# Four score banks of each middle block exponentiated on VectorE instead of ScalarE

## The chip, the cores and the metric

The kernel runs on one core of a Trainium2 chip. The metric is the device time of one execution in microseconds. A core has TensorE (PE) for matrix products, ScalarE (ACT) for activation functions, VectorE (DVE) and GpSimd (POOL) for elementwise work, and SyncE (SP), which here issues the DMAs. PE writes only to PSUM, which has 8 banks of 128 x 512 float32; the other data lie in SBUF.

## The reference

x is 2048 x 448 (bfloat16), with 16 heads of 28, a dense layer of 1792 in between, and an output of the same shape as x.

```python
def _A_ref(x, wqkv, wo):
    H = 16; Dh = D // H
    q, k, v = ...                      # x @ wqkv, split by heads
    scores = jnp.einsum("bhqd,bhkd->bhqk", q, k) * Dh ** -0.5
    p = _softmax(scores, axis=-1)
    o = jnp.einsum("bhqk,bhkd->bhqd", p, v)
    return o.transpose(0, 2, 1, 3).reshape(B, S, D) @ wo

def _B_ref(x, w1, b1, w2, b2):
    h = _gelu(jnp.einsum("bsd,df->bsf", x, w1) + b1)
    return jnp.einsum("bsf,fd->bsd", h, w2) + b2

xn = _layernorm(x)
return x + _A_ref(xn, wqkv, wo) * _silu(_B_ref(xn, w1, b1, w2, b2))
```

## The kernel before

**Attention.** The 16 heads form 4 groups of 4 (G), the 2048 queries 4 chunks of 512 (C), the 2048 keys 16 tiles of 128 (T). A *block* is one group with one chunk, 16 blocks in all. A block has 64 score *banks*, numbered m: 16 key tiles by 4 heads, each 128 keys x 512 queries. In all there are 1024 banks. The last block is cut into four quarters of the queries.

Banks are taken in *units*: pairs in block 0, threes afterwards (UB = 3). For each unit, `p_scores` (L903) has PE write its scores into the ring, 6 PSUM banks, so two units of three fit; `p_exps` (L932) has ACT exponentiate the whole unit in one instruction into slots of P (21 slots in SBUF); `p_pv` (L969) has PE multiply these with V, adding into the PSUM bank acc over the 16 key tiles. V has a column of twos, which gives the softmax denominators. No maximum is subtracted per row; a bound on the scores is folded into q and k. At the end of a block `p_epi` copies acc to SBUF on DVE (L1016), takes reciprocals (L1026) and multiplies them in (L1045), with small matmuls between.

**Filling.** One PSUM bank, misc, is left for everything else once PV has started. Through it go, tile by tile, the projections of k and q (`t_proj` L591; DVE evictions L602, L747, L757), of v (L771, L781), the first dense layer (`p_f1`: PE L811, DVE L824, 56 tiles), the second (`p_f2`: PE L854, DVE L859, 16 tiles), and the output projection (L1055, DVE L1064 and L1066). When all 56 tiles of the first layer are there, ACT runs gelu over them in four instructions (L836). `p_silu` gives the gate by a tanh on ACT (L868) and a product on DVE (L871). The output is projection x gate (L1064) plus x (L1066), then stored from SP.

**Order.** Every engine has one fixed order of instructions, laid out by a planner before the run. Each process (`p_...`) is a generator that yields tasks with an engine, buffers read and written, a planned duration and a rank; the planner puts next what can start first, and among tasks of one engine that can start within 0.1 us of one another the one of lowest rank. Scores have rank 1, exponentials 3, evictions of the first layer 2, PV 6 (1.2 when it lags more than four units), filling matmuls 5. `deps` turns the buffers into semaphore waits: an instruction waits for the last write of what it reads, and for the last write and all reads since of what it writes. What PE itself wrote is not waited for on PE. x stays in SBUF from the load at the start (`x_sb`) until L1066.

Of the kernel before, what the change touches and what calls it, by code (L numbers as in the profile page):

```python
# [6 lines left out]
dt = mybir.dt  # L7
ACTF = mybir.ActivationFunctionType
ALU = mybir.AluOpType
# [5 lines left out]
D = 448  # L15
# [4 lines left out]
C = 4  # L20
# [4 lines left out]
UB = 3  # L25
NRING = 6
NP = 21
NBLK = G * C
MTOT = NBLK * T * 4

UNITS = []
for _m in range(0, 64, 2):
    UNITS.append(([_m, _m + 1], _m % 4, _m % 20))
for _m in range(64, MTOT, UB):
    UNITS.append((list(range(_m, _m + UB)), (_m - 64) % NRING, (_m - 64) % NP))
NU = len(UNITS)
RB = {m: b0 + k for ms, b0, p0 in UNITS for k, m in enumerate(ms)}
PB = {m: p0 + k for ms, b0, p0 in UNITS for k, m in enumerate(ms)}
SM_SCALE = DH ** -0.5
LN_EPS = 1e-5  # L40
KNORM = 2.5
PV_START = 8
# [26 lines left out]
class _Kernel:  # L69
# [164 lines left out]
    def alloc(self):  # L234
# [57 lines left out]
        self.b_acc, self.b_misc = B(), B()  # L292
        self.b_P = [B() for _ in range(NP)]
        self.b_x = [B() for _ in range(C)]
        self.b_xn = [[B() for _ in range(4)] for _ in range(3)]
        self.b_xnT = [[B(), B()] for _ in range(C)]
        self.b_wqkf = B()
# [24 lines left out]
        self.b_rf = [B(), B()]  # L322
        self.banks = [(self.misc[:, :], self.b_misc), (self.acc[:, :], self.b_acc)]
        self.s_x = [self.sem("s_x%d" % q) for q in range(4)]
        self.s_out = [self.sem("s_out%d" % q) for q in range(10)]
        self.s_w = {n: self.sem("s_" + n) for n in ("wqk", "wv", "w1", "w2", "wo", "b")}

    def schedule(self):
        K = self
        K.n_f1 = 0  # L330
        K.exp_u = -1
        K.sc_u = -1
        K.pv_u = -1
        K.E_done = -1
        K.norms_done = False
        K.stg_done = 0
        K.qsqs = [0, 1]
# [9 lines left out]
        K.ring_busy = [False] * NRING  # L347
        K.P_busy = [False] * NP
# [12 lines left out]
        K.spawn(K.p_exps(), 0)  # L361
        K.spawn(K.p_pv(), 0)
        o = 1.0
# [500 lines left out]
    def p_silu(self, c):  # L864
        K = self
        yield ("until", lambda: K.f2n[c] == 4 and K.ready([K.b_fsb[c % 2]], 0.3) and (c < 2 or K.g_done[c - 2]))
        fb, sg = K.fsb[:, c % 2, :, :], K.sig[:, c % 2, :, :]
        yield _Task(ACT, lambda eng: eng.activation(sg, fb, ACTF.Tanh, scale=0.5),  # L868
                    [K.b_fsb[c % 2]], [K.b_sig[c % 2]], 1.6, 0.0, 0)
        for t in range(4):  # L870
            yield _Task(DVE, lambda eng, t=t: eng.scalar_tensor_tensor(K.g_sb[:, c, t, :], sg[:, t, :], 1.0, fb[:, t, :],  # L871
                                                                       op0=ALU.add, op1=ALU.mult),
                        [K.b_sig[c % 2], K.b_fsb[c % 2]], [K.b_h[c], K.b_g[c]], 0.63, 0.0, 6)
        K.g_done[c] = True

    def pieces(self, m):
        b, r = m // 64, m % 64
# [11 lines left out]
    def p_scores(self):  # L889
        K = self  # L890
        for u in range(NU):
            ms = UNITS[u][0]
            fl, rd = [], []
            ps = [(m,) + K.pieces(m) for m in ms]
            for k in range(4):
                for m, b, j, pc, _, _ in ps:
                    if k >= len(pc):
                        continue
                    t, q0, nq, col = pc[k]
                    g, c = b // C, b % C  # L900

                    def f(eng, m=m, t=t, j=j, g=g, c=c, q0=q0, nq=nq, col=col):
                        return eng.matmul(K.ring[:, RB[m], col:col + nq],  # L903
                                          K.kT[32 * j:32 * j + 32, g, t * 128:(t + 1) * 128],
                                          K.qT[32 * j:32 * j + 32, g, c * 512 + q0:c * 512 + q0 + nq],
                                          tile_position=(32 * j, 0), start=True, stop=True)
# [11 lines left out]
            yield ("until", lambda: not any(K.ring_busy[RB[m]] for m in ms))  # L918
            yield _Task(PE, fall, rd, [K.b_ring[RB[m]] for m in ms], 0.17 + 0.05 * len(ms) + 0.02 * (len(fl) - len(ms)), 0.1, 1)
            for m in ms:  # L920
                K.ring_busy[RB[m]] = True
            K.sc_u = u

    def p_exps(self):
        K = self
        for u in range(NU):
            ms, b0, p0 = UNITS[u]
            n = len(ms)
            yield ("until", lambda: K.sc_u >= u and not any(K.P_busy[p0 + k] for k in range(n)))

            def fexp(eng, b0=b0, p0=p0, n=n):
                return eng.activation(K.P[:, p0:p0 + n, :], K.ring[:, b0:b0 + n, :], ACTF.Exp, scale=SM_SCALE)  # L932
            yield _Task(ACT, fexp, [K.b_ring[b0 + k] for k in range(n)], [K.b_P[p0 + k] for k in range(n)],
                        0.0843 + 0.4267 * n, 0.08, 3)
            for k in range(n):
                K.ring_busy[b0 + k] = False
                K.P_busy[p0 + k] = True
            K.exp_u = u
            if u >= NU - 2:
                for k in range(n):  # L940
                    K.banks.append((K.ring[:, b0 + k, :], K.b_ring[b0 + k]))

    def p_pv(self):
        K = self
# [2 lines left out]
        K.banks.pop(i)  # L947
        K.pv_started = True
        for u in range(NU):
            ms = UNITS[u][0]  # L950
            parts, cur = [], []
            for m in ms:
                cur.append(m)
# [4 lines left out]
            for part in parts:  # L958
                if not part:
                    continue  # L960
                first = K.sub_of(part[0])
                yield ("until", lambda: K.exp_u >= u and K.E_done >= first - 1)
                fl, rd = [], []
                for m in part:
                    b, j, pc, end, s = K.pieces(m)
# [15 lines left out]
                yield _Task(PE, fall, rd, [K.b_acc], 0.18 + 0.05 * len(part) + 0.02 * (len(fl) - len(part)), 0.1,  # L981
                            lambda: 1.2 if K.exp_u - K.pv_u > 4 else 6)
                for m in part:
                    K.P_busy[PB[m]] = False
# [75 lines left out]
    def t_oev(self, ps, tok, c, t):  # L1060
# [2 lines left out]
        wr = K.b_osb[c][t // 2] if c < C - 1 else K.b_o4[t]  # L1063
        yield _Task(DVE, lambda eng: eng.tensor_tensor(o, ps, K.g_sb[:, c, t, :], ALU.mult),  # L1064
                    [tok, K.b_g[c]], [wr], 0.63, 0.0, 3)
        yield _Task(DVE, lambda eng: eng.tensor_tensor(o, o, K.x_sb[:, c, t, :], ALU.add),  # L1066
                    [K.b_x[c], wr], [wr], 0.4, 0.0, 3)
# [78 lines left out]
```

## Time and profile before

| | |
|---|---|
| median of 3 runs | 531.56 us (528.48 to 532.66) |
| the profiled execution | 530.83 us, its span 529.0 us |
| mean granted PE clock | 0.894 |
| busy, PE / DVE / ACT / POOL | 466.3 / 172.5 / 502.8 / 64.1 us |
| exponentials on ACT | 352 instructions, 461.8 us |
| gelu on ACT | 4 instructions, 24.4 us |
| DMA | 9.13 MB |

The page of the profile is one execution of the program. Busy time counts overlapping instructions of one engine once, so a group's busy time can be less than its count times its mean. The forty slices are the span in equal parts of 13.2 us, with the busy share in tenths. A group of instructions is given by source line, engine, operation and tile, with busy us, the mean ns of one, and the idle time of the engine just before it with what ended it. `acc<-P,vaug` means that acc is written from P and vaug.

### The profile page before, as it was taken

The numbers are of one execution on the slowest core, as the hardware profiler recorded it, in microseconds if no ns is written. First come the engines' busy times: TensorE is split into PE (matmuls) and PEld (weight loads), VectorE is DVE, ScalarE is ACT, GpSimd is POOL, SyncE is SP. The second block draws the span as 40 slices with busy tenths as digits, with TensorE's granted clock in tenths as the row PEclk, the third lists the DMA queues.
The fourth block names the chain that finished last, engine by engine and source line by source line (L and its number), as shares of the span: only waits on it lengthen the run. The fifth ranks groups of instructions, "written<-read, shape, count | busy, mean of one in ns | idle before, by whom it ended". The sixth has DMA issues, their size and how long they took to land.

```text
span 529.0 us, 8343 instructions
## 1 busy us (share of the span) xinstructions
PE 466.3 (88%) x3478; PEld 149.9 (28%) x3507; DVE 172.5 (33%) x304; ACT 502.8 (95%) x385; POOL 64.1 (12%) x93
## 2 busy tenths in 40 slices
PE   6899899899989999989976799999878889898984
PEld 2433233222222222222221333333212112121542
DVE  6823433343433343343433132313400003031244
ACT  3898999999999999999999799999999999999993
POOL 5662101210101001010111001000101000010100
PEclk9999999999999999999995999999955558566698
DMA  8800000000000000000000000000000000000010
GB/s 238 245 16 18 0 1 1 0 1 1 1 1 1 0 1 2 1 1 1 0 1 0 0 2 1 1 0 1 1 0 2 0 1 35 1 14 22 2 46 27
DMA packets 7925, 9.13 MB, mean 17 GB/s; under 512 B 2384, under 2 KB 6928, under 8 KB 7888
## 3 DMA queue, kind: packets, MB, share of 16 engines
q1 hardware_dynamic: 7888, 8.61, 5.3%
q8 instruction: 27, 0.44, 0.3%
q14 instruction: 10, 0.08, 0.0%
HBM read 6.77 MB, written 1.84 MB: 16 GB/s over the span
## 4 chain that ended last, share of the span: by engine, by line
ACT 44%; PE 36%; issue 14%; DVE 5%; ACTq 0%; DVEq 0%
ACT P L932 44%; PE ring L903 8%; PE misc L854 8%; PE acc L969 7%; PE misc L591 3%; PE misc L1055 2%; PE acc L678 2%; PE misc L771 1%; PE misc L1040 1%; DVE h L1064 1%; DVE qT L747 1%; PE misc L811 1%; DVE qT L757 1%; DVE h L871 1%; PE ring L591 1%
## 5 line engine op out<-in xcount | busy, mean ns | idle before, releaser
L932 ACT ACTIVATE P<-ring 128x1536 bf16<-128x1536 f32 (+1 forms) x352 | 461.8, 1644 | 7.3 <-PE ring L903 4.7
L903 PE MATMUL ring<-qT,kT 32*128 32x512 bf16 (+1 forms) x1216 | 151.4, 386 | 31.7 <-ACT P L932 29.2
L969 PE MATMUL acc<-P,vaug 128*32 128x512 bf16 (+1 forms) x1216 | 145.5, 390 | 0.0
L903 PEld LDWEIGHTS ring<-qT,kT 32*128 32x128 bf16 x1216 | 38.1, 94 | 156.6 <-ACT P L932 132.0
L824 DVE TENSOR_SCALAR h<-misc,b1c 128x512 bf16<-128x512 f32 x56 | 42.0, 751 | 80.4 <-PE misc L811 80.4
L811 PE MATMUL misc<-xnT,w 128*128 128x512 bf16 x209 | 58.8, 382 | 3.3 <-issue 1.3
L969 PEld LDWEIGHTS acc<-P,vaug 128*32 128x32 bf16 x1216 | 35.6, 96 | 83.5 <-issue 80.6
L854 PE MATMUL misc<-w,h 128*128 128x448 bf16 x224 | 52.5, 362 | 3.7 <-DVE qT L757 2.0
L1030 POOL CAST rhi<-rc 128x512 bf16<-128x512 f32 x15 | 9.1, 609 | 306.6 <-DVE rc L1026 223.8
L1016 DVE CAST E_sb<-acc 128x512 bf16<-128x512 f32 x15 | 10.3, 687 | 79.6 <-PE acc L969 79.6
L752 POOL TENSOR_TENSOR qsq<-qT 128x512 bf16<-128x512 bf16 x15 | 15.6, 1039 | 113.1 <-DVE qT L747 113.1
L859 DVE TENSOR_TENSOR w<-misc,b2b 128x448 bf16<-128x448 f32 x16 | 10.0, 622 | 54.3 <-PE misc L854 54.3
L854 PEld LDWEIGHTS misc<-w,h 128*128 128x128 bf16 x224 | 18.1, 99 | 28.4 <-issue 11.3
L836 ACT ACTIVATE h<-h 128x7168 bf16<-128x7168 bf16 x4 | 24.4, 6163 | 0.0
L811 PEld LDWEIGHTS misc<-xnT,w 128*128 128x128 bf16 x224 | 15.5, 97 | 30.2 <-issue 9.6
L591 PE MATMUL misc<-xnT,wq 128*128 128x512 bf16 x53 | 15.7, 418 | 3.0 <-DVE qT L757 2.5
L591 PE MATMUL misc<-xnT,wk 128*128 128x512 bf16 x47 | 14.9, 424 | 3.9 <-DVE qT L747 2.8
L1045 DVE TENSOR_TENSOR qT<-misc,E_sb 128x512 bf16<-128x512 f32 x15 | 10.4, 691 | 21.4 <-PE misc L1040 21.4
L747 DVE CAST qT<-misc 128x512 bf16<-128x512 f32 x14 | 9.7, 691 | 20.2 <-PE misc L591 20.2
L1031 POOL TENSOR_TENSOR rlo<-rc,rhi 128x512 bf16<-128x512 f32 x15 | 16.0, 1064 | 1.2
L602 DVE TENSOR_SCALAR kT<-misc,ecol 128x512 bf16<-128x512 f32 x13 | 9.8, 750 | 19.3 <-PE misc L591 19.3
L1055 PE MATMUL misc<-wo,qT 128*128 128x448 bf16 x56 | 15.1, 371 | 0.8 <-DVE w L1004 0.4
(119 smaller groups left out, 245.7 us busy)
## 6 DMA issues: line engine op xcount, KB each, us to landing
x_sb<-in_A_x_dram SPq DMA_DIRECT2D x4, 448.0 KB, 6.7
w<-in_B_w_dram SPq DMA_DIRECT2D x1, 1568.0 KB, 13.0
w<-in_B_w_dram SPq DMA_DIRECT2D x1, 1344.0 KB, 7.5
out_dram<-h SPq DMA_DIRECT2D x6, 224.0 KB, 2.0
h<-in_A_wqkv_dram SPq DMA_DIRECT2D x1, 672.0 KB, 4.8
out_dram<-h SPq DMA_DIRECT2D x4, 112.0 KB, 1.7
wo<-in_A_wo_dram SPq DMA_DIRECT2D x16, 24.5 KB
wv<-in_A_wqkv_dram SPq DMA_DIRECT2D x1, 336.0 KB, 5.7
```

The lines of the kernel that those rows point to most:

```text
L591: ins = eng.matmul(bank, w[:, kt, g * 128:(g + 1) * 128], K.xnT[:, kt, c * 512:(c + 1) * 512], start=(kt == 0), stop=(kt == KT - 1))
L747: yield _Task(DVE, lambda eng: eng.tensor_copy(qb, bank), [tok], [qr], 0.7, 0.0, 2)
L752: yield _Task(POOL, lambda eng: eng.tensor_tensor(qs, qb, qb, ALU.mult), [qr], [tq], 1.05, 0.0, 0)
L811: ins = eng.matmul(bank, K.w1[:, kt, ft * 128:(ft + 1) * 128], K.xnT[:, kt, c * 512:(c + 1) * 512], start=(kt == 0), stop=(kt == KT - 1))
L824: yield _Task(DVE, lambda eng: eng.tensor_scalar(dst, bank, K.b1c[:, ft:ft + 1], None, op0=ALU.add), [tok, K.b_b1c], wr, 0.75, 0.0, 2)
L836: return eng.activation(hv, hv, ACTF.Gelu_apprx_tanh)
L854: ins = eng.matmul(ps, hv[:, ft, t * 128:(t + 1) * 128], K.w2[:, ft, :], start=(ft == 0), stop=(ft == FT - 1))
L903: return eng.matmul(K.ring[:, RB[m], col:col + nq], K.kT[32 * j:32 * j + 32, g, t * 128:(t + 1) * 128], K.qT[32 * j:32 * j + 32, g, c * 51 ...
L932: return eng.activation(K.P[:, p0:p0 + n, :], K.ring[:, b0:b0 + n, :], ACTF.Exp, scale=SM_SCALE)
L969: return eng.matmul(K.acc[32 * j:32 * j + 32, q0:q0 + nq], K.vaug[:, t, 4 * g + j, :], K.P[:, PB[m], col:col + nq], tile_position=(0, 32 * ...
L1031: yield _Task(En, lambda eng: eng.tensor_tensor(K.rlo[:, :, :], rcb, K.rhi[:, :, :], ALU.subtract), [K.b_rc, K.b_rhl], [K.b_rhl], d2, 0.0, 1)
L1055: ins = eng.matmul(ps, K.qT[:, g, c * 512 + t * 128:c * 512 + (t + 1) * 128], K.wo[:, g, :], start=(g == 0), stop=(g == G - 1))
```

## The change

In blocks 1 to 14, four banks of the 64 become *late* (m = 64 b + 5, 17, 29, 41, each moved forward to the third bank of its unit). The unit's instruction on ACT then covers two banks instead of three. The late bank is exponentiated on DVE: `p_late` reads it from the ring as an int32, scaled by 65536 log2(e) / sqrt(28) and biased by 127 x 65536, so that the upper 16 bits are the exponent and the lower 16 the fraction; `p_exp2` scales the lower halves to float32, makes a quartic in three two-operand instructions, and adds the scaled int32 to it, written as uint16 whose bits are a bfloat16. A late bank has a slot of its own (`plate`, four of them) and its own PV matmul, at any place between the block's first four PV matmuls and its last part, which waits for all four (`late_left`). P's 21 slots are numbered anew, since a unit may take two. `ring_busy` and `P_busy` become per-bank flags.

The buffers of the new instructions take the room of `x_sb` once layer norm is done, so x is loaded again, by quarters, into a part of `h` that is free when a quarter's gate is done (`p_silu`), and L1066 reads that.

```diff
+LATE = set()
+for _b in range(1, NBLK - 1):
+    for _r in (5, 17, 29, 41):
+        _m = 64 * _b + _r
+        while (_m - 64) % UB != UB - 1:
+            _m += 1
+        LATE.add(_m)
...
+        xf = self.x_sb[:, :, :, :].rearrange("p c t d -> p (c t d)")
+        self.ysb = [xf[:, 1024 * i:1024 * (i + 1)].bitcast(dt.int32) for i in range(3)]
...
+        self.ev, self.eu = (xf[:, 3072 + 1024 * i:4096 + 1024 * i].bitcast(f32) for i in range(2))
+        self.plate = [xf[:, 5120 + 512 * i:5632 + 512 * i] for i in range(4)]
+        self.x2 = self.h[:, :, 3584:5376].rearrange("p c (t d) -> p c t d", d=D)
...
         K.g_done[c] = True
+        K.b_x2[c].r = list(K.b_h[c].r) + [K.b_h[c].w]
+        K.dma(SP, lambda eng: eng.dma_start(K.x2[:, c, :, :], K.A_x[0].rearrange("(c p t) d -> c p t d", p=128, t=4)[c]),
+              K.s_x2[c], writes=[K.b_x2[c]])
...
+    def p_late(self):
+        K = self
+        yield ("until", lambda: K.ln_done == 2 * C)
...
+                yield ("until", lambda: K.sc_u >= u and len(K.ys) > 0)
+                i = K.ys.pop(0)
+                yield _Task(DVE, lambda eng, m=m, i=i: eng.tensor_scalar(
+                    K.ysb[i], K.ring[:, RB[m], :], SM_SCALE * LOG2E * 65536.0, 127.0 * 65536.0, op0=ALU.mult, op1=ALU.add),
+                            [K.b_ring[RB[m]]], [K.b_y[i]], 0.72, 0.0, 1)
+                K.ring_rel[m] = True
+                K.spawn(K.p_exp2(m, i), m)
+
+    def p_exp2(self, m, i):
+        K = self
+        yield ("until", lambda: K.ln2e == 0 and len(K.pls) > 0)
+        K.ln2e = 1
+        k = K.pls.pop(0)
+        v, u, y, lo = K.ev, K.eu, K.ysb[i], K.ylo[i]
+        tv, tu, ty = K.b_ev, K.b_eu, K.b_y[i]
+        yield _Task(DVE, lambda eng: eng.tensor_scalar(v, lo, EXP_SC / 65536.0, None, op0=ALU.mult), [ty], [tv], 0.7, 0.0, 4)
+        yield _Task(DVE, lambda eng: eng.scalar_tensor_tensor(u, v, EXP_A, v, op0=ALU.add, op1=ALU.mult),
+                    [tv], [tu], 0.75, 0.0, 4)
+        yield _Task(DVE, lambda eng: eng.scalar_tensor_tensor(u, u, EXP_B, u, op0=ALU.add, op1=ALU.mult),
+                    [tu], [tu], 0.75, 0.0, 4)
+        yield _Task(DVE, lambda eng: eng.scalar_tensor_tensor(u, v, EXP_D, u, op0=ALU.mult, op1=ALU.add),
+                    [tv, tu], [tu], 0.75, 0.0, 4)
+        yield _Task(DVE, lambda eng: eng.scalar_tensor_tensor(K.plate[k].bitcast(dt.uint16), y, 2.0 ** -9, u,
+                                                              op0=ALU.mult, op1=ALU.add),
+                    [ty, tu], [K.b_pl[k]], 0.75, 0.0, 4)
+        K.ln2e = 0
+        K.ys.append(i)
+        b, j, pc, end, s = K.pieces(m)
+        g, t = b // C, pc[0][0]
+        yield ("until", lambda: K.pv_done[64 * b + 3] and K.ready([K.b_pl[k]], 0.1))
+        yield _Task(PE, lambda eng: eng.matmul(K.acc[32 * j:32 * j + 32, :], K.vaug[:, t, 4 * g + j, :], K.plate[k],
+                                               tile_position=(0, 32 * j), start=False, stop=False, skip_group_check=True),
+                    [K.b_pl[k], K.b_v[0 if g == 0 else 1][t]], [K.b_acc], 0.25, 0.1, 1.2)
+        K.pls.append(k)
+        K.late_left[b] -= 1
...
-                yield ("until", lambda: K.exp_u >= u and K.E_done >= first - 1)
+                yield ("until", lambda: K.exp_u >= u and K.E_done >= first - 1 and (
+                    not K.pieces(part[-1])[3] or K.late_left[part[-1] // 64] == 0))
...
-        yield _Task(DVE, lambda eng: eng.tensor_tensor(o, o, K.x_sb[:, c, t, :], ALU.add),
-                    [K.b_x[c], wr], [wr], 0.4, 0.0, 3)
+        yield _Task(DVE, lambda eng: eng.tensor_tensor(o, o, K.x2[:, c, t, :], ALU.add),
+                    [K.b_x2[c], wr], [wr], 0.4, 0.0, 3)
```

More of the change, by code (lines that the diff above doesn't have):

```diff
@@ L29 @@
 MTOT = NBLK * T * 4
[L31 to L35, printed above, removed]
+LATE = set()
[5 more added lines that the diff above has]
+        LATE.add(_m)
+UNITS, RB, PB, RPREV, PPREV = [], {}, {}, {}, {}
+_last, _plast, _p = {}, {}, 0
+for _m in list(range(0, 64, 2)) + list(range(64, MTOT, UB)):
+    _ms = list(range(_m, _m + (2 if _m < 64 else UB)))
+    _b0 = _m % 4 if _m < 64 else (_m - 64) % NRING
+    _na = len([m for m in _ms if m not in LATE])
+    if _p + _na > NP:
+        _p = 0
+    UNITS.append((_ms, _ms[:_na], _b0, _p))
+    for _k, m in enumerate(_ms):
+        RB[m] = _b0 + _k
+        RPREV[m] = _last.get(RB[m])
+        _last[RB[m]] = m
+        if _k < _na:
+            PB[m] = _p + _k
+            PPREV[m] = _plast.get(PB[m])
+            _plast[PB[m]] = m
+    _p += _na
 NU = len(UNITS)
-RB = {m: b0 + k for ms, b0, p0 in UNITS for k, m in enumerate(ms)}
-PB = {m: p0 + k for ms, b0, p0 in UNITS for k, m in enumerate(ms)}
 SM_SCALE = DH ** -0.5
+LOG2E = 1.4426950408889634
+EXP_SC, EXP_A, EXP_B, EXP_D = 1.1449707906804418, 2.2275165815584925, 18.59640770523752, -75.73931899211772
 LN_EPS = 1e-5
@@ L324, in alloc @@
         self.s_x = [self.sem("s_x%d" % q) for q in range(4)]
+        self.s_x2 = [self.sem("s_x2%d" % q) for q in range(4)]
         self.s_out = [self.sem("s_out%d" % q) for q in range(10)]
@@ L346, in schedule @@
         K.taken = 0
-        K.ring_busy = [False] * NRING
-        K.P_busy = [False] * NP
+        K.ring_rel = [False] * MTOT
+        K.pv_done = [False] * MTOT
+        K.late_left = [len([m for m in LATE if m // 64 == b]) for b in range(NBLK)]
+        K.ys, K.pls = [0, 1, 2], [0, 1, 2, 3]
+        K.ln2e = 0
         K.banks += [(K.ring[:, b, :], K.b_ring[b]) for b in (5, 4)]
@@ L362, in schedule @@
         K.spawn(K.p_pv(), 0)
+        K.spawn(K.p_late(), 0)
         o = 1.0
@@ L917, in p_scores @@
                 K.ring6 = True
-            yield ("until", lambda: not any(K.ring_busy[RB[m]] for m in ms))
+            yield ("until", lambda: all(RPREV[m] is None or K.ring_rel[RPREV[m]] for m in ms))
             yield _Task(PE, fall, rd, [K.b_ring[RB[m]] for m in ms], 0.17 + 0.05 * len(ms) + 0.02 * (len(fl) - len(ms)), 0.1, 1)
-            for m in ms:
-                K.ring_busy[RB[m]] = True
             K.sc_u = u
@@ L926, in p_exps @@
         for u in range(NU):
-            ms, b0, p0 = UNITS[u]
+            _, ms, b0, p0 = UNITS[u]
             n = len(ms)
-            yield ("until", lambda: K.sc_u >= u and not any(K.P_busy[p0 + k] for k in range(n)))
+            yield ("until", lambda: K.sc_u >= u and all(PPREV[m] is None or K.pv_done[PPREV[m]] for m in ms))
             def fexp(eng, b0=b0, p0=p0, n=n):
@@ L934, in p_exps @@
                         0.0843 + 0.4267 * n, 0.08, 3)
-            for k in range(n):
-                K.ring_busy[b0 + k] = False
-                K.P_busy[p0 + k] = True
+            for m in ms:
+                K.ring_rel[m] = True
             K.exp_u = u
@@ L941, in p_exps @@
                     K.banks.append((K.ring[:, b0 + k, :], K.b_ring[b0 + k]))
+    def p_late(self):
+        K = self
+        yield ("until", lambda: K.ln_done == 2 * C)
+        for b in K.b_y + K.b_pl + [K.b_ev, K.b_eu]:
+            for x in K.b_x:
+                b.r += x.r
+        for u in range(NU):
+            for m in UNITS[u][0]:
+                if m not in LATE:
+                    continue
+                yield ("until", lambda: K.sc_u >= u and len(K.ys) > 0)
[3 more added lines that the diff above has]
+                            [K.b_ring[RB[m]]], [K.b_y[i]], 0.72, 0.0, 1)
+                K.ring_rel[m] = True
+                K.spawn(K.p_exp2(m, i), m)
@@ new lines, in p_exp2 @@
+    def p_exp2(self, m, i):
[15 more added lines that the diff above has]
+                    [ty, tu], [K.b_pl[k]], 0.75, 0.0, 4)
+        K.ln2e = 0
+        K.ys.append(i)
[7 more added lines that the diff above has]
+        K.late_left[b] -= 1
@@ L949, in p_pv @@
         for u in range(NU):
-            ms = UNITS[u][0]
+            ms = UNITS[u][1]
             parts, cur = [], []
@@ L983, in p_pv @@
                 for m in part:
-                    K.P_busy[PB[m]] = False
+                    K.pv_done[m] = True
                 if end:
```

5 lines of the change are left out of this document (added).

## The prediction

> **What bounds the kernel now.** I read the busy shares and slices first, then the groups with their shapes kept apart, then ScalarE's (ACT's) own order of time, then 20 us windows.
>
> ```profile
> span 529.0 us, 8343 instructions
> PE 466.3 (88%) x3478; PEld 149.9 (28%) x3507; DVE 172.5 (33%) x304; ACT 502.8 (95%) x385; POOL 64.1 (12%) x93
> PE   6899899899989999989976799999878889898984
> DVE  6823433343433343343433132313400003031244
> ACT  3898999999999999999999799999999999999993
> PEclk9999999999999999999995999999955558566698
> ```
>
> ACT is at 9 in nearly every slice, VectorE (DVE) at 3 or 4 in the first half and almost idle late. Of ACT's 502.8 us, the exponentials take 431.7 + 30.1:
>
> ```profile
> L932 ACT ACTIVATE P<-ring 128x1536 bf16<-128x1536 f32 x320 | 431.7, 1706 | 6.8 <-PE ring L903 4.4 <-PE acc L969 2.1
> L932 ACT ACTIVATE P<-ring 128x1024 bf16<-128x1024 f32 x32 | 30.1, 1028 | 0.4 <-PE ring L903 0.3
> L836 ACT ACTIVATE h<-h 128x7168 bf16<-128x7168 bf16 x4 | 24.4, 6163 | 0.0
> ```
>
> The means (1706, 1028 ns) overlap one another, since 320 x 1706 would be 546 us; what counts is the distance from one start to the next. ACT's order of time gives it in unbroken runs:
>
> ```profile
> 27.30 12.32 ACT L932 ACTIVATE P<-ring 128x1024 bf16<-128x1024 f32 x13
> 51.47 217.72 ACT L932 ACTIVATE P<-ring 128x1536 bf16<-128x1536 f32 x162 [2.10 <-PE acc L969]
> 301.89 8.46 ACT L932 ACTIVATE P<-ring 128x1536 bf16<-128x1536 f32 x6 [2.90 <-PE ring L903]
> 379.76 60.98 ACT L932 ACTIVATE P<-ring 128x1536 bf16<-128x1536 f32 x45
> 471.97 48.66 ACT L932 ACTIVATE P<-ring 128x1536 bf16<-128x1536 f32 x36 [0.65 <-PE ring L903]
> ```
>
> Three banks: (217.72 - 1.71) / 161 = **1.342 us** a step. Two banks: (12.32 - 1.03) / 12 = **0.941 us**. ACT waits 6.8 us in all before its 320 large exponentials. So ACT paces this kernel from about 20 us to 520 us, and a block of 64 banks takes 21.33 x 1.342 = 28.6 us.
>
> **What goes.** The change names 4 banks in each of blocks 1 to 14, 56 in all, each the third of its unit, so 56 units step at 0.941 instead of 1.342: 56 x 0.401 = **22.5 us** off ACT. Nothing else on ACT changes. That is the most there is to win: 530.83 - 22.5 = 508.3 for the profiled execution (span 529.0, 1.8 us around it), which lies 0.7 below the median of the three runs, 531.56.
>
> **What DVE gets.** Per late bank: one PSUM read to int32, one scaling of the low halves to float32, four two-operand instructions on float32 or int32. No row shows float32 operands in SBUF. The nearest:
>
> ```profile
> L824 DVE TENSOR_SCALAR h<-misc,b1c x56: 749/751/753, 105.4 to 267.0; 128x512 bf16<-128x512 f32 x56
> L757 DVE SCALAR_TENSOR_TENSOR qT<-misc,colK,qT 128x512 bf16<-128x512 f32 x15 | 11.3, 751 | 9.3 <-PE misc L754 6.4 <-PE acc L969 2.3 <-PE misc L854 0.6
> L1045 DVE TENSOR_TENSOR qT<-misc,E_sb 128x512 bf16<-128x512 f32 x15 | 10.4, 691 | 21.4 <-PE misc L1040 21.4
> L871 DVE SCALAR_TENSOR_TENSOR h<-w x16: 615/624/1351, 312.0 to 382.8; 128x448 bf16<-128x448 bf16 x16
> L1064 DVE TENSOR_TENSOR h<-misc,h x14: 623/624/625, 441.0 to 518.0; 128x448 bf16<-128x448 f32 x14
> L553 DVE TENSOR_SCALAR h<-x_sb,mv,rstd 128x448 bf16<-128x448 bf16 x4 | 1.5, 390 | 0.4 <-ACT rstd L544 0.4
> 525.85 0.62 DVE L1064 TENSOR_TENSOR h<-ring,h 128x448 bf16<-128x448 f32 x1 [0.46 <-PE ring L1055]
> 526.50 0.39 DVE L1066 TENSOR_TENSOR h<-h,x_sb 128x448 bf16<-128x448 bf16 x1
> ```
>
> L871 has no per-partition scalar and takes 0.624 at 448 elements, as L1064 does; L1045 takes 0.691 at 512; L824 and L757, with such a scalar, 0.751. The new ones have constants only, so I take 0.69 for the read (0.69 to 0.75) and for each of the four (0.69 to 0.96, the upper end being three eighths above it, from nothing nearer). The scaling has a row at 0.39 (L553, 16 bit to 16 bit, dense) and one at 0.75; its input is strided and its output float32, less like L553, so I take 0.69. A dependent DVE instruction starts 0.03 us after the end before it (525.85 + 0.62 to 526.50). Sum: 6 x 0.69 + 5 x 0.03 = **4.3 us** a late bank; from both sides 4.0 to 5.5. The planner that lays the order out has 4.42 for it (0.72 + 0.7 + 4 x 0.75).
>
> The Trainium skill (VectorE: DVE Perf Modes, "The perf-mode tier table") says a tensor_scalar from SBUF runs float32 at two elements a cycle, which would make the scaling an estimated 0.42 and the chain 4.0; the same table allows two float32 tensors one element a cycle. No row here shows either.
>
> 56 x 4.3 = 241 us on top of 172.5: DVE at 413 of some 510. Not over, but in the stage that fills TensorE (PE) with projections and the first dense layer it is close:
>
> ```profile
> 140.00:160.00 20.00, 17.85 (x130) 5.53 (x133) 6.98 (x11) 20.00 (x17) 2.69 (x3) 1.00 0.00 1
> 220.00:240.00 20.00, 18.29 (x132) 5.48 (x134) 7.61 (x11) 20.00 (x16) 1.66 (x2) 1.00 0.00 1
> 400.00:420.00 20.00, 18.00 (x102) 4.15 (x102) 1.64 (x3) 19.92 (x16) 1.66 (x2) 0.50 0.00 1
> 150.08 0.75 DVE L824 TENSOR_SCALAR h<-misc,b1c 128x512 bf16<-128x512 f32 x1 [1.24 <-PE misc L811]
> 152.44 0.75 DVE L824 TENSOR_SCALAR h<-misc,b1c 128x512 bf16<-128x512 f32 x1 [1.61 <-PE misc L811]
> 154.76 0.75 DVE L824 TENSOR_SCALAR h<-misc,b1c 128x512 bf16<-128x512 f32 x1 [1.56 <-PE misc L811]
> ```
>
> Columns: PE, weight loads, DVE, ACT, POOL, then granted clock. DVE works 7.0 to 7.6 of 20 us there, 10.4 a block; a new block is 28.6 - 4 x 0.40 = 27.0 us. 10.4 + 4 x 4.3 = 27.6. So DVE is **just full** in the filling stage. What gives way? Filling goes through one free bank (misc): two pairs of matmuls, one eviction, every 2.35 us (150.08, 152.44, 154.76), DVE idle 1.6 between. A ready chain instruction is taken in that gap; three of them where 1.6 us holds two push the eviction to 3.0 us. The chain gets three of four slots, 6 instructions in 6 us, 24 a block: it keeps up, and filling slows by about a quarter. That costs nothing while there is room behind it:
>
> ```profile
> L859 DVE TENSOR_TENSOR w<-misc,b2b x16: 612/624/625, 295.1 to 377.3; 128x448 bf16<-128x448 f32 x16
> ```
>
> Filling ends at 383 (L871's last), its product is first used at 441 (L1064's first), and only the last quarter is needed near 500. 56 first-layer evictions at +0.65 are 36 us, some some 45 of q, k and v at half of that, for their shorter waits, 13, the second layer's sixteen at 0.4 another 6: 55 us later, 438. Twelve output tiles at the 2.4 us of a first-layer tile fit behind that before 500. If the cover is gone, each us lands on the end.
>
> **Waits added.** (a) Scores for a unit wait for DVE's read of the late bank two units before, and the ring's next exponential waits for them. Scores are ready 0.5 us after the bank is free (below), then 1.34 - 0.5 of the exponential before and 0.94 of their own: 1.78 us for an instruction in progress (0.75) and the read (0.69). It holds; behind it in DVE's order stand evictions, for which PE's fill waits. (b) The last PV (probabilities times V) of a block waits for the four late PVs; behind it in PE's order stand scores. The last late bank is 20 banks ahead of the end, 6.7 units or 8.9 us, for a chain of 4.3 and one queued; P's 21 slots cover about 9 us more. (c) The step after a two-bank exponential.
>
> ```profile
> 149.98 0.39 PE L903 MATMUL ring<-qT,kT 32*128 32x512 bf16 x3
> 150.30 0.40 PE L969 MATMUL acc<-P,vaug 128*32 128x512 bf16 x3
> ...
> 152.71 0.61 PE L969 MATMUL acc<-P,vaug 128*32 128x512 bf16 x6
> 153.25 0.61 PE L811 MATMUL misc<-xnT,w 128*128 128x512 bf16 x2
> ...
> 404.16 0.61 PE L903 MATMUL ring<-qT,kT 32*128 32x512 bf16 x3 [0.19 <-ACT P L932]
> 404.70 0.61 PE L969 MATMUL acc<-P,vaug 128*32 128x512 bf16 x2
> 405.35 0.69 DVE L1016 CAST E_sb<-acc 128x512 bf16<-128x512 f32 x1 [21.33 <-PE acc L969]
> 405.50 0.61 PE L903 MATMUL ring<-qT,kT 32*128 32x512 bf16 x3 [0.19 <-ACT P L932]
> ```
>
> Scores take 0.39 and a hop below 0.1 (404.70 + 0.61 to 405.35), so 0.5 of a 1.34 step leaves 0.84 for PE to finish what it is at; of a 0.94 step, 0.44. A fill pair (0.61) or a doubled PV (0.61) begun just before overruns by up to 0.17; where clock is 0.50 (400 to 420) scores take 0.61 and a PV 0.61 after it, overrun up to 0.4. Mean between nothing and that, for 56 units: 0 to 16 us; I take 0.09, **5 us**, since most releases find PE between pieces.
>
> **On PE.** Each late PV is a matmul of its own: beside another PV it overlaps (six in 0.61, three in 0.40), alone it adds the distance from pack to pack, 0.32 at full clock (149.98 to 150.30), 0.54 at half. 0 to 56 x 0.54 = 30 us of PE, under filling's room until 383 and in the gaps after (PE 18.00 of 20 at 400). No time taken.
>
> **DMA.** Four reloads of x, 448 KB each; the first load's row:
>
> ```profile
> x_sb<-in_A_x_dram SPq DMA_DIRECT2D x4, 448.0 KB, 6.7
> ```
>
> They are issued on SP after each quarter's gate is done (up to 383, shifted to 438), read from 441 on; 6.7 us is hidden. Behind them on SP stand only output stores, which come later. Cover gone, 6.7 us at the end.
>
> **Sum:** 530.83 - 22.5 + 5 = 513.3; by the median, **514**.
>
> **Rivals.** (1) *DVE paces the filling stage.* Its 27.6 against 27.0 us a block is no margin, and the order is fixed before the run: any late eviction holds a chain and through it a ring bank. Blocks 1 to 8 then win nothing, 24 late banks win 24 x 0.40 = 9.6, less 2: 523. For: the sum above. Against: the chain may take the slots and fill can slide. (2) *The change moves time but ends nothing*: the freed 0.40 us turns into a wait for scores, overrun 0.17 to 0.4 at every late unit and a stall at block ends. 530, from 526 to 536. Against: thirteen two-bank steps ran unbroken at 0.941 with the clock full. (3) *Slower: the chain costs more than the order allows for.* Place: blocks 1 to 9, DVE. The order gives 4.42 a late bank; at c the block grows by 4 (c - 4.42) and gains 1.6. With the 7.6 won later, it decides at 9 x (4 (c - 4.42) - 1.6) = 7.6, c = 5.0 us, 0.81 an instruction. At 0.9 (c = 0.69 + 5 x 0.93 = 5.3): 9 x 1.9 - 7.6 = +10, 541; at 0.96, 550. For: no row has float32 from SBUF. Against: rows without a scalar operand sit at 0.69. (4) *Half clock while filling.* The clock is 0.50 at 400 to 420 with PE busy 18.00 of 20, full at 140 to 160 with 17.85: what differs is that fill matmuls (128 rows) are gone. Sparser fill could halve it earlier; fill from 51 to 383 at 1.5 times lasts to 549, and the tail after it to 560. The Trainium skill (TensorE: Matmul & The Clock Gate, "What's actually happening") has the gate follow how busy PE was lately; the trace's 18.00 of 20 at half clock doesn't agree by busy time alone, so I keep its chance small.
>
> **Chances.** Forecast (507 to 519) 0.53; rival 1 (519 to 526) 0.19; rival 2 0.14; rival 3 0.11; rival 4 0.03. About 1% (5.3 us) is what a measurement tells from no change. Faster 0.72, same 0.14, slower 0.14. The range takes the forecast, rival 1 and rival 2 up to 532, some 0.80; its low end is the full 22.5 with 1 us of noise. A float32 price between 4.0 and 4.8 a chain lies inside it.
>
> **What would show it.** Exponentials: 264 of three banks, 88 of two, steps still 1.34 and 0.94. DVE busy about 410, chain instructions near 0.69. ACT's idle before exponentials, 6.8 now, near 12. First-layer evictions further apart than 2.35 us and their last later than 267. If ACT's idle names DVE or grows above 20, or a chain instruction takes over 0.8, the forecast is wrong.

## The result, and the profile after

The changed kernel takes **507.67 us** (median of 4 runs, 507.18 to 509.05) against 532.11 before (4 runs, 528.48 to 533.15): ratio 0.9563, 95% interval 0.9512 to 0.9614. The forecast was 514, in a range from 507 to 532: the time lies inside it, 0.7 us above its low end.

The page of the changed kernel, its busy shares and slices:

```profile
span 505.4 us, 8696 instructions
PE 452.5 (90%) x3507; PEld 146.0 (29%) x3507; DVE 379.0 (75%) x640; ACT 478.8 (95%) x385; POOL 74.2 (15%) x93
PE   6899899998999999999999999766999999999884
DVE  6823997879688898988888888832576868588545
ACT  3899999999999999999999999997899999999993
PEclk9999999999699999999999999956999999999989
```

ACT is as full as it was and 24.0 us shorter (502.8 to 478.8); the span is 23.6 shorter. DVE went from 33% to 75% and fills almost the whole middle. The slow stretch of PE's clock before (5 and 6 in seven of the last ten slices) is gone.

The groups of the changed kernel with their shapes kept apart (count | busy us, mean ns of one | idle before, releasers):

```profile
L969 ACT ACTIVATE P<-ring 128x1536 bf16<-128x1536 f32 x264 | 368.4, 1590 | 7.3 <-PE ring L942 7.0
L969 ACT ACTIVATE P<-ring 128x1024 bf16<-128x1024 f32 x88 | 96.1, 1123 | 0.4 <-PE ring L942 0.3
L991 DVE TENSOR_SCALAR x_sb<-ring 128x512 int32<-128x512 f32 x56 | 38.6, 689 | 17.4 <-PE ring L942 16.3
L1004 DVE TENSOR_SCALAR x_sb<-x_sb 128x512 f32<-128x512 uint16 x56 | 24.4, 436 | 0.2
L1005 DVE SCALAR_TENSOR_TENSOR x_sb<-x_sb 128x512 f32<-128x512 f32 x56 | 41.8, 746 | 1.0
L1007 DVE SCALAR_TENSOR_TENSOR x_sb<-x_sb 128x512 f32<-128x512 f32 x56 | 40.7, 727 | 1.1
L1009 DVE SCALAR_TENSOR_TENSOR x_sb<-x_sb 128x512 f32<-128x512 f32 x56 | 40.9, 730 | 0.9
L1011 DVE SCALAR_TENSOR_TENSOR x_sb<-x_sb 128x512 uint16<-128x512 int32 x56 | 41.1, 734 | 1.0
```

264 and 88 exponentials, as the change says; the idle time in front of them is 7.7 us, 7.2 before. A chain is 0.689 + 0.436 + 0.746 + 0.727 + 0.730 + 0.734 = **4.06 us** of DVE. From the starts of the single exponentials, the median distance after one of three banks is 1.330 us, after one of two 0.904, so a bank is worth 0.426 us: 56 x 0.426 = 23.9. Here is what is lost of it. Timeline of the changed kernel around one of the late units:

```profile
76.83 2.62 ACT L969 ACTIVATE P<-ring 128x1536 bf16<-128x1536 f32 x2
78.26 0.82 PE L807 MATMUL misc<-wv,xnT 128*128 128x384 bf16 x4
79.01 0.39 PE L942 MATMUL ring<-qT,kT 32*128 32x512 bf16 x3
79.45 1.45 ACT L969 ACTIVATE P<-ring 128x1536 bf16<-128x1536 f32 x1
```

The second of the two exponentials on the first line is the one of two banks, at 78.16. PE is at four matmuls for v until 79.0, only then come the scores, and the next exponential starts at 79.45, 0.05 after they end: a step of 1.29 instead of 0.90. Of the 56 steps that follow a late unit, 54 are under 1.6 us and have a mean of 0.975, so they lose 54 x 0.071 = 3.8 us in all. One at 131.6 us loses 1.3, and one behind gelu (349.6) loses 4.9, where the like step before lost 3.0.

Two windows of 20 us (PE, weight loads, DVE, ACT, POOL, granted clock), in the filling stage and where the clock had been 0.50 before:

```profile
220.00:240.00 20.00, 19.20 (x138) 5.30 (x136) 17.22 (x28) 20.00 (x17) 2.69 (x2) 1.00 0.00 1
400.00:420.00 20.00, 19.84 (x143) 6.34 (x142) 14.15 (x24) 20.00 (x17) 1.87 (x2) 1.00 0.09 25
```

DVE has 17.2 of 20 us there, so 2.8 to spare. Filling lasts longer: lines L860 (first layer), L907 (gates) and L1147 (outputs), with first and last start, of the changed kernel:

```profile
L860 DVE TENSOR_SCALAR h<-misc,b1c x56: 734/749/753, 127.4 to 319.6; 128x512 bf16<-128x512 f32 x56
L907 DVE SCALAR_TENSOR_TENSOR h<-w x16: 562/624/626, 374.8 to 471.5; 128x448 bf16<-128x448 bf16 x16
L1147 DVE TENSOR_TENSOR h<-misc,h x13: 609/625/626, 451.8 to 493.7; 128x448 bf16<-128x448 f32 x13
```

The first layer ends 53 us later than before (267.0), the last gate 89 us later (382.8). Outputs begin at 451.8 and the last quarter's after 471.5, still ahead of the last exponential, which ends at 496.6. PE thus has wide matmuls to do where it had none, and in those windows the clock is full.

### The profile page after: what moved, and what is told of

It reads as the page before. It is cut to its first block, busy times and chain, and to the rows that moved or that the text cites. A ratio compares the mean times of both kernels' runs of the same rounds, so it can differ in the third digit from the quotient of the medians.

```text
span 505.4 us, 8696 instructions
## 1 busy us (share of the span) xinstructions
PE 452.5 (90%) x3507; PEld 146.0 (29%) x3507; DVE 379.0 (75%) x640; ACT 478.8 (95%) x385; POOL 74.2 (15%) x93
## 4 chain that ended last, share of the span: by engine, by line
PE 39%; ACT 38%; issue 15%; DVE 7%; ACTq 0%; DVEq 0%
ACT P L969 38%; PE ring L942 9%; PE misc L890 9%; PE acc L1052 7%; PE misc L627 3%; PE misc L847 3%; PE acc L714 1%; PE acc L1019 1%; DVE qT L793 1%; DVE qT L783 1%; PE ring L627 1%; DVE w L1087 1%; DVE x_sb L1009 1%; DVE x_sb L991 1%; PE ring L807 1%
## 5 line engine op out<-in xcount | busy, mean ns | idle before, releaser
L969 ACT ACTIVATE P<-ring 128x1536 bf16<-128x1536 f32 (+1 forms) x352 | 438.0, 1473 | 7.7 <-PE ring L942 7.4
L942 PE MATMUL ring<-qT,kT 32*128 32x512 bf16 (+1 forms) x1216 | 139.1, 355 | 25.6 <-ACT P L969 20.9
L1052 PE MATMUL acc<-P,vaug 128*32 128x512 bf16 (+1 forms) x1160 | 130.9, 355 | 0.0
L847 PE MATMUL misc<-xnT,w 128*128 128x512 bf16 x224 | 63.5, 388 | 0.4 <-DVE qT L793 0.2
L991 DVE TENSOR_SCALAR x_sb<-ring 128x512 int32<-128x512 f32 x56 | 38.6, 689 | 17.4 <-PE ring L942 16.3
L860 DVE TENSOR_SCALAR h<-misc,b1c 128x512 bf16<-128x512 f32 x56 | 41.8, 747 | 11.8 <-PE misc L847 11.4
L1113 POOL CAST rhi<-rc 128x512 bf16<-128x512 f32 x15 | 13.4, 891 | 245.0 <-DVE rc L1109 169.8
L1005 DVE SCALAR_TENSOR_TENSOR x_sb<-x_sb 128x512 f32<-128x512 f32 x56 | 41.8, 746 | 1.0
L1011 DVE SCALAR_TENSOR_TENSOR x_sb<-x_sb 128x512 uint16<-128x512 int32 x56 | 41.1, 734 | 1.0
L1009 DVE SCALAR_TENSOR_TENSOR x_sb<-x_sb 128x512 f32<-128x512 f32 x56 | 40.9, 730 | 0.9
L1007 DVE SCALAR_TENSOR_TENSOR x_sb<-x_sb 128x512 f32<-128x512 f32 x56 | 40.7, 727 | 1.1
L890 PEld LDWEIGHTS misc<-w,h 128*128 128x128 bf16 x224 | 17.2, 99 | 28.9 <-issue 14.7
L1004 DVE TENSOR_SCALAR x_sb<-x_sb 128x512 f32<-128x512 uint16 x56 | 24.4, 436 | 0.2
L872 ACT ACTIVATE h<-h 128x7168 bf16<-128x7168 bf16 x4 | 24.4, 6164 | 0.0
L1019 PE MATMUL acc<-x_sb,vaug 128*32 128x512 bf16 x56 | 21.9, 392 | 0.2 <-DVE x_sb L1011 0.2
```

Of the source, the lines that this page charges most:

```text
L847: ins = eng.matmul(bank, K.w1[:, kt, ft * 128:(ft + 1) * 128], K.xnT[:, kt, c * 512:(c + 1) * 512], start=(kt == 0), stop=(kt == KT - 1))
L860: yield _Task(DVE, lambda eng: eng.tensor_scalar(dst, bank, K.b1c[:, ft:ft + 1], None, op0=ALU.add), [tok, K.b_b1c], wr, 0.75, 0.0, 2)
L890: ins = eng.matmul(ps, hv[:, ft, t * 128:(t + 1) * 128], K.w2[:, ft, :], start=(ft == 0), stop=(ft == FT - 1))
L942: return eng.matmul(K.ring[:, RB[m], col:col + nq], K.kT[32 * j:32 * j + 32, g, t * 128:(t + 1) * 128], K.qT[32 * j:32 * j + 32, g, c * 51 ...
L991: yield _Task(DVE, lambda eng, m=m, i=i: eng.tensor_scalar(K.ysb[i], K.ring[:, RB[m], :], SM_SCALE * LOG2E * 65536.0, 127.0 * 65536.0, op0 ...
L1005: yield _Task(DVE, lambda eng: eng.scalar_tensor_tensor(u, v, EXP_A, v, op0=ALU.add, op1=ALU.mult), [tv], [tu], 0.75, 0.0, 4)
```

## The experiments

The theory: *the time is ACT's steps; each late bank is worth the same wherever it lies, and the chain on DVE is hidden as long as DVE is not full.* Rival 1 of the prediction: DVE paces the filling stage. A new rival 2, another than the prediction's: the gain is PE's clock, kept full by the longer filling. Four kernels:

**The reload of x alone**

```diff
-for _b in range(1, NBLK - 1):
+for _b in range(0):
```

> No late banks at all; left of the change are the reload of x and the new numbering of P's slots. Theory (ACT's shorter steps are the gain): as before, 531 to 533 us, x's reload hidden. Rival (clock): as before too, since the filling ends where it did, with the granted clock at 0.5 after about 383 us. Rival (the reload or the slots cost or bring something): away from 532 by 2 us or more.

Measured: 530.53 us, ratio 0.9974 (0.9940 to 1.0008). No difference that can be told. The new slots do one thing by themselves that its trace shows: ACT's step into block 1 takes 1.52 us instead of 3.13, because the wait of 2.10 us for PV there (the prediction's line at 51.47) is gone.

**Late banks in blocks 1 to 8 alone**

```diff
-for _b in range(1, NBLK - 1):
+for _b in range(1, 9):
```

> Late banks in blocks 1 to 8 alone, 32 of the 56. Theory: each late bank is worth the same, 24.4 / 56 = 0.436 us, so 532 - 14 = 518 us. Rival 1 (VectorE paces the filling stage): 528 to 530, these blocks bring next to nothing. Rival 2 (the gain is TensorE's clock, kept up by filling that lasts longer): 508 to 512, since the filling still slides.

Measured: 518.27 us, ratio 0.9761 (0.9725 to 0.9796). Against the 531.4 of before in the same series, 13.1 us for 32 banks, 0.41 each (0.34 to 0.46 by the interval). The filling stage, where DVE is fullest, gives its whole share: rival 1 falls, and this isn't the 508 to 512 of rival 2.

**Late banks in blocks 9 to 14 alone**

```diff
-for _b in range(1, NBLK - 1):
+for _b in range(9, NBLK - 1):
```

> Late banks in blocks 9 to 14 alone, 24 of the 56. Theory: 24 x 0.436 = 10.5, so 521.5 us, with the clock back at 0.5 in a stretch after the filling. Rival 1 (VectorE paces the filling stage): 510 to 512, nearly all of the gain. Rival 2 (clock): 528 to 531, because the filling ends early and the clock falls.

Measured: 521.82 us, ratio 0.9812 (0.9761 to 0.9864). 9.6 us for 24 banks, 0.40 each (0.30 to 0.53 by the interval: a gain, though not surely one of over 2%); the two halves add up to 22.7 of the 24.4. Rival 2 expected 528 or more, and its condition was met. The last gate is at 393.4, and then the clock falls, in this kernel's window

```profile
400.00:420.00 20.00, 16.97 (x98) 3.46 (x97) 12.23 (x20) 19.18 (x16) 0.00 (x0) 0.67 0.00 1
```

to 0.67, and stays at 0.66 to 0.81 until 500. What the low clock costs can also be read from the trace before: from 385 us on, ACT's steps lost 3.6 us in all against 1.330 each, and 2.1 us in the changed kernel. Single runs of before do go with the clock (527.38 us at a mean of 0.911, 533.25 at 0.885), so a few us of any difference can be the clock's, but not the 24.

**The quartic left out**

```diff
-        yield _Task(DVE, ... scalar_tensor_tensor(u, v, EXP_A, v, ...)
-        yield _Task(DVE, ... scalar_tensor_tensor(u, u, EXP_B, u, ...)
-        yield _Task(DVE, ... scalar_tensor_tensor(u, v, EXP_D, u, ...)
+        u, tu = v, tv
```

> All 56 late banks, but the three two-operand instructions of the quartic are left out, so their values are not exponentials; a chain is 3 instructions, about 1.9 us instead of 4.1. Theory: VectorE's chain is hidden, 507 to 508 us, with the last first-layer eviction earlier than 319.6 by 20 us or more. Rival 1 (VectorE still costs): 503 us or less, ACT's waits after two-bank exponentials gone. Rival 2 (clock): 512 or more, for the filling ends earlier and the clock falls sooner.

The busy shares of the kernel without the quartic, and its clock:

```profile
PE 447.9 (89%) x3475; PEld 148.1 (29%) x3507; DVE 267.7 (53%) x472; ACT 479.7 (95%) x385; POOL 67.7 (13%) x93
PEclk9999999999999999999999999999999988576688
```

Measured: 505.32 us, ratio 0.9528 (0.9482 to 0.9574). 111 us less on DVE (379.0 to 267.7) bring 2 us, and the intervals of the two ratios overlap. The chain is hidden all but a little. The last first-layer eviction is at 287.0, 33 us earlier, as forecast; ACT's losses after late units stay (4.3 us in 54 steps), so they aren't the chain's. The clock falls again after the last gate (413.3), to 0.67 to 0.83 between 400 and 480, and the time doesn't rise: rival 2 falls here too.

Two pairs then ask **how far the cover reaches**, by more late banks and by a longer chain.

**One more instruction in each chain, and two more**

```diff
+        for _ in range(1):      # in the second kernel, range(2)
+            yield _Task(DVE, ... scalar_tensor_tensor(u, v, EXP_A, v, ...), [tv], [tu], 0.0, 0.0, 4)
         yield _Task(DVE, ... scalar_tensor_tensor(u, v, EXP_A, v, ...), [tv], [tu], 0.75, 0.0, 4)
```

> Four late banks a block; each chain has its first quartic instruction twice (same result), planned at no time, so a chain is 4.1 + 0.75 and the order of instructions hardly moves. Rival 3 of the prediction has its point at a chain of 5.0: by it this one, at 4.9, would be at 527 to 531 us. By the rows, VectorE at 17.4 + 2.3 of 20 us in the filling stage still just fits: 508 to 513 us.

> As the one with one more, but with the instruction three times, a chain of 5.7. VectorE would have 17.4 + 4.4 of 20 us in the filling stage, so it paces blocks 1 to 10 by some 9%: 10 x 2.4 = 24 us above 508, 525 to 535. Prediction's rival 3 at 5.7: 9 x (4 x 1.28 - 1.6) - 7.6 = 24 above 531, 555. If the chain doesn't matter at all: 508.

Measured: 510.73 us with one more (508.63 to 510.95 in three of its four runs, 517.02 in the other; ratio 0.965, 0.9585 to 0.9715) and **552.77** with two more (1.0394, 1.0367 to 1.0421). At a chain of some 4.8 us it costs at most little, as the rows said and not rival 3; at 5.5 the change is a loss of 4%, near rival 3's 555 and not the 525 to 535 by the rows. The same window of the kernel with one more, and of that with two:

```profile
200.00:220.00 20.00, 17.57 (x119) 4.76 (x119) 19.08 (x30) 19.92 (x17) 1.15 (x1) 1.00 0.01 1
200.00:220.00 20.00, 14.50 (x113) 4.51 (x113) 19.25 (x30) 17.72 (x15) 2.65 (x3) 1.00 0.00 1
```

and a line of the waits with two more (us in total, times, longest):

```profile
ACT P L969 <- PE ring L942: 41.5, 57, 7.9
```

DVE is at 19.08 and at 19.25 of 20, so it is as good as full in both. With one more, ACT still has its 19.92; with two more it has 17.72 and waits 41.5 us for scores, in 57 places. The same order of instructions, laid out for 4.42 a chain, holds at 4.8 and runs late everywhere at 5.5.

How full DVE is shows over blocks 3 to 8 as a whole, from the first exponential of block 3 to that of block 9. It is busy 23.3 us of a block's 27.2 in the changed kernel, 25.6 of 27.5 with one more and 28.6 of 30.6 with two more: 93% of the block is the most it reaches in these kernels. Its work besides the chains, durations added up, is 8.7, 8.5 and 8.2 us a block there, with 38, 37 and 33 first-layer evictions in the six blocks. So part of it slides to later blocks as the chains grow.

**Five late banks a block, and six**

```diff
-    for _r in (5, 17, 29, 41):
+    for _r in (4, 14, 24, 34, 44):         # the second kernel: (4, 12, 20, 28, 36, 44)
```

> Five late banks a block instead of four (from places 4, 14, 24, 34, 44), 70 in all. If ACT still sets the time: 531.5 - 70 x 0.436 = 501 us. If VectorE or the filling behind it takes over: VectorE would have about 17.4 + 3 of 20 us in the filling stage, the last gate, at 471 us of 505 with four, slides by 30 us to the end, and the time stays at 507 or rises to 515.

> Six late banks a block, 84 in all. If ACT still sets the time: 495 us. If VectorE and the filling set it: VectorE's work is 379 + 28 x 4.2 = 497 us, more than fits beside its waits, and the time rises to 515 to 530.

Measured: **564.36 us** with five (ratio 1.0622, 1.0601 to 1.0644), **634.89** with six (1.1941, 1.1909 to 1.1973). Far beyond what either theory expected. Waits of the kernel with five:

```profile
ACT P L969 <- PE ring L942: 25.4, 14, 16.7
ACT P L969 <- PE acc L1052: 25.2, 7, 6.6
```

Two kinds: 25.4 us for scores, 16.7 of it at one place, and 25.2 at the ends of blocks, for PV. The one place, in the same kernel's timeline:

```profile
288.51 1.45 PE L627 MATMUL misc<-xnT,wk 128*128 128x512 bf16 x4 [0.31 <-DVE h L860]
290.80 0.60 PE L942 MATMUL ring<-qT,kT 32*128 32x512 bf16 x6 [0.85 <-DVE kT L638]
291.24 41.45 ACT L969 ACTIVATE P<-ring 128x1536 bf16<-128x1536 f32 x33 [16.71 <-PE ring L942]
```

Scores of block 8 wait for the last tile of its k, which is projected at 288; before the change it lay in kT at 186, in the changed kernel at 223. Why so late? The first layer's matmuls in this kernel, by their line, and then the copy of its bias in DVE's timeline:

```profile
L847 PE MATMUL misc<-xnT,w x209: 377/379/634, 122.6 to 379.0; 128*128 128x512 bf16 x105
```

```profile
187.73 0.17 DVE L853 CAST b1c<-b1s 128x14 f32<-128x14 bf16 x1
```

The first tile's matmuls come at 122.6; its eviction needs the bias copy, a task of 0.17 us with the default rank 5. Chain instructions have rank 4, and the planner, it seems, always had one ready with five chains a block. So the copy waits **65 us**, and with it the one bank through which k, q and the first layer go: PE's matmuls write misc at 123.7 and next at 190.6. In the changed kernel the same copy is at 127.13, 9 us after the first matmuls at 118.2; with six late banks at 232.8. To test that, one rank was changed, with five late banks and with four:

```diff
-  ... eng.tensor_copy(K.b1c[:, :], K.b1s[:, :]), [K.b_b1], [K.b_b1c], 0.17)
+  ... eng.tensor_copy(K.b1c[:, :], K.b1s[:, :]), [K.b_b1], [K.b_b1c], 0.17, 0.05, 2)
```

> Five late banks a block, and one more edit: the single copy of the first layer's bias (0.17 us on VectorE) gets rank 2 instead of 5, so that chain instructions (rank 4) no longer go before it. With five late banks it came at 187.7 us, 65 us after the first matmuls whose bank waits for it. Theory A (the cliff is that copy, which holds the one bank of the filling): the filling goes on at once and the time falls from 564 to 502 to 512 us. Theory B (VectorE is simply full): the copy moves and the time stays within 10 us of 564.

> The change as it is, four late banks a block, with the bias copy at rank 2: it came at 127.1 us, 9 us after the first matmuls at 118.2. Theory (ACT sets the time, filling has room): the same within 2 us, 505 to 509, with the first layer's end some 8 us earlier than 320. Rival (the filling's lateness sets the end, with the last gate at 471): 500 us.

Measured with five: 546.16 us (ratio 1.0294, 1.0242 to 1.0346). Both theories miss: the copy is at 123.49 and 18 us come back, but not the other 40 down to 505. What is left, in the waits of this kernel:

```profile
ACT P L969 <- PE acc L1052: 36.4, 9, 7.1
ACT P L969 <- PE ring L942: 12.3, 18, 2.7
```

Now it is the ends of blocks: P has no free slot, since the block's last PV waits for its last late bank (at the end of block 3 the last chain ends at 149.6, its PV starts at 150.9, and ACT goes on at 152.1 after 7.1 us of waiting). Measured with four: **504.29 us** (503.83 to 504.42; ratio 0.9495, 0.9462 to 0.9529). It is the fastest of all kernels here; its runs lie below the changed kernel's 507.18 to 509.05, but the ratio intervals overlap, and the two were not in one series. It came out between the two expectations. Its first layer ends 14 us earlier (305.9).

Last, both with two more edits, so that DVE loses nothing to ranks or wrong costs:

```diff
-  [K.b_sig[c % 2], K.b_fsb[c % 2]], [K.b_h[c], K.b_g[c]], 0.63, 0.0, 6)
+  [K.b_sig[c % 2], K.b_fsb[c % 2]], [K.b_h[c], K.b_g[c]], 0.63, 0.0, 3)
   # and in the chain, planned us: 0.72 -> 0.69, 0.7 -> 0.44, 0.75 -> 0.72
```

> Five late banks a block, the bias copy at rank 2, the gate's products (rank 6) at rank 3, and the planned costs of the chain set to the measured ones (0.69, 0.44, 4 times 0.72). Theory A: ACT's 14 further short steps bring up to 6 us against the change, 501 to 505 us. Theory B (VectorE full at 18 of 20 us): no better than 512.

> Four late banks a block with all three of these edits. If only ACT's steps count: 505 to 508 us, the last gate before 460. If VectorE's order still costs the change something: 500 to 504.

Measured: five 532.13 us (ratio 1.0023, 0.9995 to 1.0050), four 507.61 (0.9569, 0.9521 to 0.9616). What ACT still waits for with five:

```profile
ACT P L969 <- PE acc L1052: 24.2, 7, 5.7
```

Theory B has the time right for five. Blocks 3 to 8 of this kernel, from 101.6 to 288.1 us by the first exponentials of blocks 3 and 9, take 31.1 us each, where ACT alone would need 16.33 x 1.330 + 5 x 0.904 = 26.2. DVE is busy 28.9 of these 31.1 us, the same 93% as with two more instructions a chain. But its work besides the chains is 10.3 us a block, with 51 first-layer evictions in the six blocks against 38 in the changed kernel: in this order evictions (rank 2) go before the chain (rank 4), and less of the filling slides than with four. The prediction's sum with the measured chain, 10.4 + 5 x 4.06 = 30.7, therefore agrees here; with one more instruction a chain it would be 10.4 + 4 x 4.78 = 29.5, and 27.5 was measured. Whether five late banks would pay in an order in which evictions yield, no run shows.

For four, the further edits bring nothing to the time, which is that of "only ACT's steps count", though the last gate comes at 427.7 instead of 471.5 (468.4 with the copy's rank alone).

## Why the prediction was right, point by point

**ACT paces, 22.5 us to win.** Right, a little short. ACT's exponentials fell from 461.8 to 438.0. The step of two banks was read as 0.941 from a run of block 0 that holds waits; the undisturbed one is 0.904, 56 x 0.037 = 2 us more.

**5 us lost to waits after two-bank exponentials.** The mechanism was right, and the size nearly: 3.8 us in 54 steps, and 1.3 and 1.9 more in the two others. The balance was wrong, because other waits went, which the sum put at nothing. Steps from three banks lost less than before (mean 1.333 against 1.340 over 257 steps, 1.8 us), and the step into block 1 lost 1.6 us less, through the new numbers of P's slots alone. All that ACT's steps lost beyond 1.330 and 0.904, other work of ACT set aside, was 12.6 us before and 13.3 after: 0.7 more, not 5. So 23.4 of the 23.9 us came through on ACT's stretch, from the first exponential to the end of the last (17.77 to 520.63 before, 17.16 to 496.57 after), where the sum had 17.5. This term is what makes 514 instead of 508. That the time still lies in the range is due to its low end, which was the whole 22.5 and 1 us of noise.

**The chain, 4.3 us.** Measured 4.06. The two-operand instructions took 0.73 to 0.75 on the mean, but 0.69 where POOL was idle (below), as taken; the scaling took 0.436 instead of 0.69. Here the sentence on the Trainium skill (VectorE: DVE Perf Modes, "The perf-mode tier table") had the better number, an estimated 0.42 for float32 at two elements a cycle: the trace agrees, for an input of 16 bits and an output of float32.

**DVE just full at 27.6 against 27.0.** The right stage, but not the right sum: 26.6 with the measured chain, while DVE was busy only 23.3 of 27.2 us a block. The 10.4 us of other work isn't fixed, since part of the filling slides to later blocks. That is why a chain of 4.78 still fits, which the sum excludes. The margin was larger than it looked, and still small: a chain of 5.54 or a fifth bank is past it.

**Filling slides by 55 us to 438.** Wrong by 33 us: the last gate was at 471.5. (Its own terms make 57: 45 tiles at half of 0.65 are 14.6, not 13.) For the first layer the sum holds: from its first eviction to its last it takes 192 us instead of 162, 31 us more where 36 were forecast, but it also starts 22 us later, some 8 of them behind the bias copy. What failed is the rule "a ready chain instruction is taken in that gap", which the prediction worked out for evictions of rank 2 alone; the gate's products (rank 6) and the bias copy (rank 5) yield to every chain. With both ranks raised, and the chain's planned costs with them, the last gate is at 427.7 with four late banks. The room, to 500, held all the same.

**Rivals.** 1 fell with blocks 1 to 8 alone (0.41 us a bank). The prediction's 2 fell with the result. 3 did not come, but its mechanism is real: its point was a chain of 5.0, and the runs put it between 4.8 (510.73) and 5.5 (552.77). Its price fits past the point alone: at the measured chain of 5.54 it gives 18 us above before, and 21 were measured; at 4.78 it gives 522, and 510.73 was measured. (Its 550 for 0.96 an instruction should be 553 by its own formula.) 4 went the other way: while the filling lasted the clock stayed full, 0.965 on the mean against 0.894. Its last argument, that busy time alone doesn't explain the gate, is weaker than it looks (see the end).

**Signs.** 264 and 88 exponentials, steps of 1.33 and 0.90, and later, sparser evictions came as said. DVE's busy time was 379 where about 410 was expected, and ACT's idle time before exponentials 7.7 where near 12 was, which is the term of 5 us again.

**What it did not see** is the second way to the same cliff: a low-ranked task of 0.17 us that holds the only bank. With five late banks it was worth 18 of the 33 us by which that kernel is slower than before.

## What to carry to other kernels

When one engine paces and another idles at a third, moving a piece over is worth the pacing engine's step for that piece, wherever it lies, until the other engine is full in the fullest stage (here at 93% of a block); look at that stage and not at the whole span, and ask which of its work there can slide. Just past that point the loss is many times the gain per piece (here a fifth bank a block could have won 6 us, and cost 57; 25 with ranks and costs mended). And in an order made by ranks, a queue of new work that is never empty starves everything ranked below it: look for short tasks there that hold a buffer.

## What the hardware showed that was not expected

DVE and POOL held one another up. DVE and POOL in the changed kernel's timeline:

```profile
68.51 0.68 DVE L1009 SCALAR_TENSOR_TENSOR x_sb<-x_sb 128x512 f32<-128x512 f32 x1
68.68 1.42 POOL L788 TENSOR_TENSOR qsq<-qT 128x512 bf16<-128x512 bf16 x1 [12.65 <-DVE qT L783]
69.23 1.41 DVE L1011 SCALAR_TENSOR_TENSOR x_sb<-x_sb 128x512 uint16<-128x512 int32 x1
```

POOL's square took 1.42 where it had a mean of 1.04 before, and DVE's last chain instruction 1.41. Over all 56, a two-operand chain instruction takes 0.686 when POOL is idle and 0.91 to 1.05 on the mean beside POOL, up to 1.5; the read from PSUM stays at 0.688 either way. The scaling, which has one input in SBUF, takes 0.418 alone and 0.56 on the mean beside POOL (7 cases). The Trainium skill (SBUF — State Buffer, "Who interferes with whom") says that a VectorE instruction with two SBUF inputs and a GpSimd instruction that reads SBUF contend for a port that one holds for its whole instruction, while one with a single SBUF input, or none, does so only in VectorE's two-port modes. The trace agrees in the main: DVE's first instruction ends at 68.51 + 0.68 = 69.19, POOL's at 70.10, and DVE's second 0.5 us later, at 70.64, a little less than its own 0.69. It made the chain some 0.2 us longer than undisturbed.

Apart from the stretch of gelu, half clock came where the filling ended. Before the change the last gate is at 382.8 and the clock 0.50 from 400 to 440, with little but scores and PV on PE; with late banks in blocks 1 to 8 alone the last gate is at 426.4 and the clock 0.51 from 440 to 460; with all of them it is at 471.5 and the clock 1.00 up to 480. PE's busy share does not tell the two apart: 18.00 of 20 us at 0.50 (400 to 420 before), 17.85 at 1.00 (140 to 160 before). But a matmul of the scores takes 603 ns at 0.50 and 385 at 1.00 (400 to 420 before and after), so those 18.00 us are an estimated 18.00 x 385 / 603 = 11.5 us at full clock. Whether the clock goes by that amount of work or by the wide matmuls, no run shows.
